# A long convolution by FFT ahead of a token-mixing layer: one weight load for all frequencies of the first transform, with x loads, spectrum loads, evictions and stores moved

## The chip, the cores and the metric

The kernel runs on one core of a Trainium2 chip. The metric is the device time of a whole run in microseconds (us). The five engines of the core work side by side: PE (TensorE, matmuls; PEld is its weight load), DVE (VectorE), ACT (ScalarE), POOL (GpSimd) and SP (SyncE, which here only issues DMAs). An *eviction* is the copy of a matmul's result out of PSUM, where PE writes it, into SBUF, the on-chip memory that the engines work from. A DMA *lands* when its data has arrived. The kernel before took 2326.43 us (median of 2 runs, 2326.23 to 2326.64).

## The reference

Two layers in a row. The first is a causal long convolution along the sequence; the second mixes tokens with two 5696 x 5696 matrices.

```python
batch, seq, d_model = 8, 5696, 128
# layer 1
L = 2 * S
y = irfft(rfft(x, n=L, axis=1) * rfft(h, n=L, axis=0)[None], n=L, axis=1)[:, :S, :]
# layer 2, with x = y
theta = x @ w_theta
zr, zi = x * cos(theta), x * sin(theta)
u = x + einsum('ts,bsd->btd', w_tok_r, zr) + einsum('ts,bsd->btd', w_tok_i, zi)
out = u + maximum(u @ w_ch, 0)
```

## The kernel before

The convolution is done by matmuls with Fourier tables, in eight *groups* (batch pair `bp`, channel half `dh`). For each group:

- **first transform** (`stage_a`): weights are the 128 sequence columns of one channel of x, the moving operand is the table `f1_t`; one half of the frequencies at a time;
- **second transform and product** (`f2`, `stage_b`): 12 chunks of frequencies, evicted by ACT, multiplied on DVE with the spectrum of h, which is loaded from HBM chunk by chunk (`hs`, four buffers);
- **inverse stage** (`stage_c`): 256 matmuls with a dense weight load each, evicted by DVE with a sign;
- **last stage** (`stage_d`): 128 matmuls, seven evictions on ACT, then the result goes to HBM.

`woven` interleaves lists of steps in program order. The first transform of group g+1 is woven into the inverse stage of group g; the product of group g+1 into the last stage of group g. Then 44 *phase steps* make zr and zi for layer 2, and a long matmul part mixes tokens.

```python
HALF = ((0, K1 // 2 + 1), (K1 // 2 + 1, K1 // 2 - 1))      # K1 = 90: 46 and 44 frequencies
fa = pool("fft_a", 2, ...);  fh = pool("fft_h", 4, ...)

def stage_a(lhs, kh, dst):                                  # for each half kh
    k0, kn = HALF[kh]
    def chunk(q):
        ...
        for i in range(8):
            nc.tensor.matmul(ps[:, i // 4, (i % 4) * 2 * kn:(i % 4 + 1) * 2 * kn],
                             lhs(q + i), f1_t[:NB, 2 * k0:2 * k0 + 2 * kn], start=True, stop=True)
        nc.scalar.activation(...)                           # eviction on ACT
    return [lambda q=q: chunk(q) for q in range(0, HD, 8)]

def lhs(q):                                                 # weights: every 128th element of a row of x16
    return x16.rearrange("p b n d -> p (b n) d")[:NB, :, dh * HD + q]

def stage_b(a_of, dh):
    def chunk(c):
        hs = fh.tile([P, 2, HD * CK], F16, tag="hs", name="hs")
        for e in range(2):
            nc.sync.dma_start(hs[64 * e:64 * e + 64], hf_hbm[dh, c])
        ps = f2(a_of, c)
        nc.scalar.activation(xs[:, :, :, :ck], ps, AF.Copy)
        for r in range(2):
            nc.vector.tensor_tensor(uv[r][:, :, :, k0:k0 + ck], xs[...], hv[:, r:r + 1, ...], op=mult)

for g, (bp, dh) in enumerate(groups):
    ...
    woven(stage_c(st), nxt, now)                            # nxt: first transform of g + 1
    if dh == 0 and bp + 1 < B // 2:
        x16s[bp + 1] = load_x(bp + 1)                       # Pool queue, one x buffer
    ...
    woven(stage_b(a_of, ...) if nxt else [], stage_d(st, bp, dh), now)

# phase step (phases_b): buffers red and mag, two of each
nc.scalar.activation(mag, r, AF.Abs)
nc.scalar.activation(red, r, AF.Sin, ...)
nc.scalar.activation(mag, mag, AF.Sin, ...)
zi_eng.tensor_mul(zi, red, yflat);  nc.vector.tensor_mul(zr, mag, yflat)
nc.sync.dma_start(...)                                      # two stores of zr, two of zi, one of y
```

Of the kernel before, what the change touches and what calls it, by code (L numbers as in the profile page):

```python
# [12 lines left out]
F16 = mybir.dt.float16  # L13
add = mybir.AluOpType.add
mult = mybir.AluOpType.mult
AF = mybir.ActivationFunctionType
# [6 lines left out]
def kernel(  # L23
# [68 lines left out]
    assert N1 * N2 == NF and NB * N2 == S and NB % 2 == 1 and K1 <= P  # L92
    HALF = ((0, K1 // 2 + 1), (K1 // 2 + 1, K1 // 2 - 1))
    CHK = [(kh, c0, min(CK, HALF[kh][1] - c0)) for kh in range(2) for c0 in range(0, HALF[kh][1], CK)]
    NCK = len(CHK) // 2
    CN = 10
    CHN = [(c0, min(CN, N2 - c0)) for c0 in range(0, N2, CN)]
    UVW = 2 * HD * K1
    hf_hbm = nc.dram_tensor("hf_hbm", (2, 2 * NCK, N2, 2, HD * CK), F16, kind="Internal").ap()
    yt_hbm = nc.dram_tensor("yt_hbm", (D, B, S), BF16, kind="Internal").ap()  # L100
# [13 lines left out]
    fc = pool("fft_c", 1, conv, side="right")  # L114
    fa = pool("fft_a", 2, conv, side="right")
    fs = pool("fft_s", 2, conv, side="right")
# [58 lines left out]
    t, k = turns_of([[1, K1]], 0, lane[:NB, 1:2], NB, N1)  # L175
    for k0, kn in HALF:
        sine(f1_t[:NB, 2 * k0 + kn:2 * k0 + 2 * kn], t[:, k0:k0 + kn], -1)
    for k0, kn in HALF:
        cosine(f1_t[:NB, 2 * k0:2 * k0 + kn], t[:, k0:k0 + kn], k[:, k0:k0 + kn])

# [9 lines left out]

    def stage_a(lhs, kh, dst):

        k0, kn = HALF[kh]
        st = {}

        def chunk(q):
            if q == 0:
                st["a"] = dst[kh] = fa.tile([P, 2 * HALF[0][1], HD], F16, tag="a", name="a_")
            ps = psum()
            for i in range(8):  # L200
                nc.tensor.matmul(ps[:, i // 4, (i % 4) * 2 * kn:(i % 4 + 1) * 2 * kn],  # L201
                                 lhs(q + i), f1_t[:NB, 2 * k0:2 * k0 + 2 * kn], start=True, stop=True)
            nc.scalar.activation(
                st["a"][:, :2 * kn, q:q + 8].rearrange("p k (a q) -> p k a q", a=2),
                ps[:, :, :8 * kn].rearrange("p a (q k) -> p k a q", q=4), AF.Copy)
        return [lambda q=q: chunk(q) for q in range(0, HD, 8)]

    def f2(a_of, c):

        kh, c0, ck = CHK[c]  # L210
        a_, (k0, kn) = a_of[kh], HALF[kh]
        ps = psum()
        for j in range(ck):
            for ri in range(2):
                for e in range(2):
                    rows = slice(64 * e, 64 * e + 64)
                    nc.tensor.matmul(ps[:, e, j * HD:(j + 1) * HD],  # L217
                                     w_t2[rows, k0 + c0 + j, N2 * (1 - ri):N2 * (3 - ri)],
                                     a_[rows, ri * kn + c0 + j, :],
                                     start=(ri == 0), stop=(ri == 1))  # L220
        return ps[:, :, :ck * HD].rearrange("p e (k d) -> p e d k", k=ck)

    def woven(*lists):

        steps = [((i + 0.5) / len(l), n, f) for n, l in enumerate(lists) for i, f in enumerate(l)]
        for _, _, f in sorted(steps, key=lambda s: s[:2]):
            f()
# [3 lines left out]
    x16s = {0: load_x(0)}  # L231
    a_h = {}
    woven([s for kh in range(2) for s in stage_a(
        lambda q: h16[:NB].rearrange("p h n d -> p (h n) d")[:, :, q], kh, a_h)],
        [lambda k0=k0: w_table(k0) for k0 in range(15, K1, 15)])

    hst = [t[:, :NCK * D * CK].rearrange("p (c h d k) -> p c h d k", c=NCK, h=2, k=CK) for t in (u_t, v_t)]
    for kh in range(2):
        nc.gpsimd.memset(hst[kh][:, NCK - 1], 0.0)

    def h_chunk(c):
        kh, c0, ck = CHK[c]
        ps = f2(a_h, c)
        dst = hst[kh][:, c % NCK, :, :, :ck]
        if c % 2:
            nc.vector.tensor_scalar(dst, ps, 16.0 / NF, None, op0=mult)  # L246
        else:
            nc.scalar.activation(dst, ps, AF.Copy, scale=16.0 / NF)
        for cc, j in ((0, 0), (2 * NCK - 1, CHK[-1][2] - 1)):
            if c == cc:  # L250
                nc.vector.tensor_scalar(dst[:, :, :, j], dst[:, :, :, j], 0.5, None, op0=mult)
        for ri in range(2):
            nc.sync.dma_start(
                hf_hbm[:, c, :, ri, :].rearrange("h p n -> p h n"),
                hst[kh][64 * ri:64 * ri + 64, c % NCK].rearrange("p h d k -> p h (d k)"))

    for c in range(2 * NCK):
        h_chunk(c)
# [32 lines left out]

    def stage_b(a_of, dh):

        def chunk(c):
            kh, c0, ck = CHK[c]
            hs = fh.tile([P, 2, HD * CK], F16, tag="hs", name="hs")
            hv = hs.rearrange("p r (d k) -> p r d k", k=CK)
            for e in range(2):
                nc.sync.dma_start(hs[64 * e:64 * e + 64], hf_hbm[dh, c])
            ps = f2(a_of, c)  # L300
            xs = fs.tile([P, 2, HD, CK], F16, tag="xs", name="xs")
            nc.scalar.activation(xs[:, :, :, :ck], ps, AF.Copy)  # L302
            k0 = HALF[kh][0] + c0
            for r in range(2):
                nc.vector.tensor_tensor(  # L305
                    uv[r][:, :, :, k0:k0 + ck], xs[:, :, :, :ck],
                    hv[:, r:r + 1, :, :ck].to_broadcast([P, 2, HD, ck]), op=mult)
        return [lambda c=c: chunk(c) for c in range(2 * NCK)]

# [16 lines left out]
    def stage_d(st, bp, dh):  # L326
        def chunk(n0, cn):
            if n0 == 0:
                st["yt"] = fg.tile([P, NB, N2], BF16, tag="yt", name="yt")
            g_, yt = st["g"], st["yt"]  # L330
            ps = psum()
            nq = 5 if cn == CN else cn
            for j in range(cn):
                n = n0 + j
                o = ps[:, j // nq, (j % nq) * NB:(j % nq + 1) * NB]
                for ri in range(2):
                    e_ = e_t[:K1, n, ri, :] if n < EN else e_t[:K1, N2 - n, ri, ::-1]
                    nc.tensor.matmul(o, g_[:K1, ri * N2 + n, :], e_, start=(ri == 0), stop=(ri == 1))
            nc.scalar.activation(  # L339
                yt[:, :, n0:n0 + cn].rearrange("p m (a q) -> p m a q", q=nq),  # L340
                ps[:, :cn // nq, :nq * NB].rearrange("p a (q m) -> p m a q", q=nq), AF.Copy)
            if n0 + cn == N2:
                for e in range(2):
                    nc.sync.dma_start(yt_hbm[dh * HD:(dh + 1) * HD, 2 * bp + e, :],
                                      yt[64 * e:64 * e + 64].rearrange("p m n -> p (m n)"))
        return [lambda n0=n0, cn=cn: chunk(n0, cn) for n0, cn in CHN]

    groups = [(bp, dh) for bp in range(B // 2) for dh in range(2)]

    def front(g):  # L350
        bp, dh = groups[g]
        a_of, x16 = {}, x16s[bp]

        def lhs(q):
            return x16.rearrange("p b n d -> p (b n) d")[:NB, :, dh * HD + q]
        return [s for kh in range(2) for s in stage_a(lhs, kh, a_of)], a_of

    a0, a_of = front(0)
    woven(a0, [lambda: r_table(0, r_u), lambda: r_table(1, r_v), s_table])
    woven(stage_b(a_of, 0), [lambda n0=n0: e_table(n0) for n0 in range(0, EN, 11)])  # L360
    setup.close()
    fg = pool("fft_g", 1, conv, side="right")

    def phases_b(ti, y_ap, b0, nb, yT, sb, th_pool, th_tag, zi_eng, turns=None, tags=("red", "mag"), m=P,
                 theta_ps=None):
        n = nb * D
# [36 lines left out]
        for r, (z, dst) in enumerate(((zr, zr_hbm), (zi, zi_hbm))):  # L403
            for e in range(2):
                t0 = ti * P + e * 64
                if t0 >= 2 * H:
                    if e == 0:
# [3 lines left out]
                i, t0 = divmod(t0, QR)  # L411
                nc.sync.dma_start(dst[p_, t0 // 64, i, :, b0 * D:b0 * D + n],
                                  z[e * 64:e * 64 + 64])
# [27 lines left out]
    def phase_step(ti, hh):  # L441
# [5 lines left out]
        for b in range(4):  # L447
# [4 lines left out]
                          y_ap.rearrange("p b d -> p (b d)"))  # L452
        phases_b(ti, y_ap, 4 * hh, 4, yT, st["sb1"], None, None, nc.vector, st["turns"], theta_ps=ps[:, 0, :])

# [5 lines left out]
    for g, (bp, dh) in enumerate(groups):  # L460
        st = {}
        last = g + 1 == len(groups)
        nxt, a_of = front(g + 1) if not last else ([], None)
        now = [steps0.pop(0) for _ in range(10)] if last else []
        woven(stage_c(st), nxt, now)
        if dh == 0 and bp + 1 < B // 2:
            x16s[bp + 1] = load_x(bp + 1)
        if g + 2 == len(groups):
# [3 lines left out]
        now = [steps0.pop(0) for _ in range(6)] if last else []  # L472
        woven(stage_b(a_of, groups[g + 1][1]) if nxt else [], stage_d(st, bp, dh), now)
    conv.close()
# [398 lines left out]
```

## Time and profile before

I cut the span into parts by the timeline (start of the first inverse matmul, its last, and so on). "Rest" is from the last inverse matmul of a group to the first one of the next: the last stage of one group with the product of the next.

| part, us | before |
|---|---|
| tables, spectrum of h, first product | 100.7 |
| inverse stages of groups 0 to 6 | 214.0 (30.5 each) |
| rests of groups 0, 2, 4 (x is loaded there) | 92.5 (30.8 each) |
| rests of groups 1, 3, 5, 6 | 84.9 |
| group 7 with 16 phase steps | 55.6 |
| last inverse-transform matmul to last of the 44 phase steps | 116.5 |
| last phase step to first sum of the mixing part | 57.5 |
| mixing part | 1605.4 |

From the page of the kernel before, the span and the chain of work that ended last (followed back from the last instruction, as shares of the span by engine and then by line):

```profile
span 2327.1 us, 42585 instructions
...
PE 62%; DMA 5%; DVE 4%; POOL 1%; issue 1%; ACT 1%; SPq 0%; DVEq 0%; ACTq 0%
PE m L812 56%; DMA wb<-in_moe_w_tok_r_dram 2%; POOL wb L534 1%; DVE c L819 1%; DMA wb<-in_moe_w_tok_i_dram 1%; DMA zr_hbm<-mag 1%; PE utp L624 1%; PE v L631 1%; PE m L773 1%; PE m L775 1%; PE m L816 1%; DVE wt L543 1%; DMA y_hbm<-yb 1%; DMA
```

The chain says that the mixing matmuls, L812, hold 56% of the span. The change leaves them alone, so the whole gain must come from the first 671 us.

Groups of instructions of the kernel before in its first 560 us (line, engine, operation, tiles, shape, count | busy us, mean ns | idle time before them and who ended it). L201 is the first transform, L320 half of the inverse stage, L305 the product:

```profile
L201 PE MATMUL ps<-f_t,x 89*128 89x88 f16 (+1 forms) x1024 | 144.7, 302 | 1.1 <-DVE v_t L246 1.0
L320 PE MATMUL ps<-r_u,u_t 128*128 128x128 f16 x1024 | 140.5, 229 | 33.6 <-DVE u_t L305 32.7 <-ACT red L396 0.3
...
L201 PEld LDWEIGHTS <-x 89*128 89x128 f16 x1024 | 136.7, 269 | 1.3 <-issue 1.1
...
L305 DVE TENSOR_TENSOR u_t<-xs,hs 128x1024 f16<-128x1024 f16 x96 | 63.9, 666 | 67.2 <-DMA hs<-hf_hbm 46.1 <-ACT xs L302 18.9 <-ACT yt L339 1.2
```

1024 loads of x keep the weight path busy for 136.7 us, 133 ns each. (The means, 269 and 302 ns, are of single overlapping instructions; busy time over count tells the pace.)

The timeline around one forward step of the kernel before (start us, duration us, instruction, count):

```profile
167.99 1.08 PEld L201 LDWEIGHTS <-x 89*128 89x128 f16 x8
168.04 1.15 PE L201 MATMUL ps<-f_t,x 89*128 89x92 f16 x8
168.24 1.35 DVE L322 TENSOR_TENSOR g__2515<-ps,sgn 90x1024 f16<-90x1024 f32 x1 [0.23 <-PE ps L321]
...
169.87 0.36 PEld L201 LDWEIGHTS <-x 89*128 89x128 f16 x2
```

Eight loads take 1.08 us without a gap. The next forward step begins 1.88 us after this one: 16 inverse matmuls, 55 ns apart, fill the rest.

Windows of the kernel before (stretch, its length, busy us and instructions of each engine, PE clock that was granted as a share of full speed, DMA share, GB/s): the inverse stage of group 2, its rest, and the phase steps alone:

```profile
core 0: us, PE busy (x) PEld busy (x) DVE busy (x) ACT busy (x) POOL busy (x), PEclk, DMA share, GB/s
213.30:243.70 30.40, 30.40 (x377) 30.25 (x378) 21.84 (x16) 11.57 (x15) 0.00 (x0) 0.94 0.28 75
243.70:274.40 30.70, 17.02 (x499) 15.45 (x497) 15.54 (x25) 16.68 (x20) 2.10 (x4) 0.67 0.82 175
583.00:660.00 77.00, 47.44 (x311) 31.78 (x310) 42.72 (x76) 40.16 (x67) 0.00 (x0) 0.63 0.58 151
```

In the inverse stage PE is busy for all of 30.4 us. In the rest no engine is: DVE works 15.5 of 30.7 us. Who made DVE wait in that rest (engine, line, releaser: us, times, longest):

```profile
DVE u_t L305 <- DMA hs<-hf_hbm: 12.3, 2, 10.6
```

DVE stood still for 10.6 us at once for a spectrum chunk, while the x load (20 us to land, issued just as the stage began) was in the DMA engines.

Timeline of SP and ACT in the kernel before, in two phase steps:

```profile
597.62 1.18 SPq L412 DMA_DIRECT2D zr_hbm<-mag  x2
...
598.46 0.60 ACT L395 ACTIVATE mag<-ps 128x512 f32<-128x512 f32 x1 [2.30 <-DMA zr_hbm<-mag]
...
598.86 0.59 SPq L412 DMA_DIRECT2D zi_hbm<-red  x1
...
599.49 1.09 SPq L451 DMA_DIRECT2D y_hbm<-y_ap  x2
...
600.37 0.60 ACT L395 ACTIVATE mag<-ps 128x512 f32<-128x512 f32 x1
600.62 0.44 SPq L652 DMA_DIRECT2D yy<-y_hbm  x1
...
601.16 1.09 SPq L412 DMA_DIRECT2D zi_hbm<-red  x2
```

SP issues without a pause, about 0.6 us for each DMA. At 598.46 ACT has waited 2.30 us for a store of zr to land and give back its buffer.

### The profile page before, as it was taken

To read this page: it belongs to the slowest core of one execution; us is meant where nothing else is said; L and a number is where in the kernel's file an instruction comes from. 1 tells how busy PE (TensorE), PEld (TensorE's weight loads), DVE (VectorE), ACT (ScalarE), POOL (GpSimd) and SP (SyncE) were. 2 spreads that over 40 slices of the span, in tenths; PEclk is the share of its full clock that TensorE was granted. 3 is DMA by queue.
4 is the path that set the end of the run, shared out by engine and by line. 5 is a ranking of instruction groups with operands and counts; after the bars stand their busy time and mean duration, and the time that the engine had idled before them with its cause. 6 is when DMAs were issued, how large, how long until landed. Compare 5 with 4: busy or idle time off the path is not lost.

```text
span 2327.1 us, 42585 instructions
## 1 busy us (share of the span) xinstructions
PE 2080.3 (89%) x16255; PEld 1187.5 (51%) x16255; DVE 1693.7 (73%) x3004; ACT 633.8 (27%) x931; POOL 842.6 (36%) x1521
## 2 busy tenths in 40 slices
PE   3778787875558999999999999799999999999997
PEld 3778787863333444444444444244444444444443
DVE  5757675774579888886888767787767777777674
ACT  5645454554532233322331000011111111111111
POOL 3300000002014445445455664345454454444540
PEclk9889798997679999999999999899999999999998
DMA  5252525358588999988999987968797787877972
GB/s 126 81 131 82 131 82 131 82 158 203 145 259 145 175 179 176 169 169 145 173 171 172 162 130 163 262 103 143 132 157 130 138 153 132 151 139 133 156 128 57
DMA packets 408989, 340.47 MB, mean 146 GB/s; under 512 B 83759, under 2 KB 366255, under 8 KB 406959
## 3 DMA queue, kind: packets, MB, share of 16 engines
q0 software_dynamic: 218240, 143.00, 45.6%
q1 hardware_dynamic: 183440, 179.41, 26.9%
q10 hardware_dynamic: 7104, 15.34, 1.9%
q8 instruction: 127, 2.08, 0.4%
q14 instruction: 78, 0.64, 0.1%
HBM read 382.55 MB, written 97.93 MB: 206 GB/s over the span
## 4 chain that ended last, share of the span: by engine, by line
PE 62%; DMA 5%; DVE 4%; POOL 1%; issue 1%; ACT 1%; SPq 0%; DVEq 0%; ACTq 0%
PE m L812 56%; DMA wb<-in_moe_w_tok_r_dram 2%; POOL wb L534 1%; DVE c L819 1%; DMA wb<-in_moe_w_tok_i_dram 1%; DMA zr_hbm<-mag 1%; PE utp L624 1%; PE v L631 1%; PE m L773 1%; PE m L775 1%; PE m L816 1%; DVE wt L543 1%; DMA y_hbm<-yb 1%; DMA b<-zr_hbm 0%; PE theta_ps L375 0%
## 5 line engine op out<-in xcount | busy, mean ns | idle before, releaser
L534 POOL DMA_DIRECT2D wb<-in_moe_w_tok_i_dram x720 | 389.9, 553 | 816.1 <-DVE wt L543 734.1
L534 POOL DMA_DIRECT2D wb<-in_moe_w_tok_r_dram x720 | 389.0, 556 | 305.3 <-ACT yt L339 188.6
L812 PE MATMUL m<-b,wt 128*128 128x512 bf16 x1936 | 454.4, 381 | 19.6 <-DVE wt L543 15.6
L543 DVE STREAM_TRANSPOSE wt<-wb 128x384 f32<-128x384 f32 (+2 forms) x720 | 359.4, 522 | 129.2 <-PE m L812 68.0
L812 PEld LDWEIGHTS <-wt 128*128 128x128 bf16 x1936 | 189.3, 98 | 254.5 <-DVE wt L543 18.6
L819 DVE TENSOR_TENSOR c<-c,m 128x512 f32<-128x512 f32 x440 | 283.2, 668 | 0.0
L626 ACT ACTIVATE uts<-utp 128x512 bf16<-128x512 bf16 (+1 forms) x90 | 53.3, 592 | 616.2 <-PE utp L624 616.2
L320 PE MATMUL ps<-r_u,u_t 128*128 128x128 f16 x1024 | 140.5, 229 | 33.6 <-DVE u_t L305 32.7
L201 PE MATMUL ps<-f_t,x 89*128 89x88 f16 (+1 forms) x1024 | 144.7, 302 | 1.1 <-DVE v_t L246 1.0
L321 PE MATMUL ps<-r_v,v_t 128*128 128x128 f16 x1024 | 137.9, 228 | 0.3
L201 PEld LDWEIGHTS <-x 89*128 89x128 f16 x1024 | 136.7, 269 | 1.3 <-issue 1.1
L320 PEld LDWEIGHTS <-u_t 128*128 128x128 f16 x1024 | 110.5, 108 | 33.8 <-DVE u_t L305 33.8
L621 ACT ACTIVATE ub<-c 128x512 bf16<-128x512 f32 (+1 forms) x90 | 56.5, 628 | 226.7 <-DMA wb<-in_moe_w_tok_i_dram 163.4
L305 DVE TENSOR_TENSOR u_t<-xs,hs 128x1024 f16<-128x1024 f16 x96 | 63.9, 666 | 67.2 <-DMA hs<-hf_hbm 46.1
L321 PEld LDWEIGHTS <-v_t 128*128 128x128 f16 x1024 | 106.5, 104 | 3.2 <-issue 1.9
L135 POOL DMA_DIRECT2D x<-in_x_dram x16 | 8.6, 542 | 266.5 <-PE ps L201 266.2
L302 ACT ACTIVATE xs<-ps 128x1024 f16<-128x1024 f32 x96 | 91.5, 986 | 48.7 <-DVE v_t L305 43.6
L217 PEld LDWEIGHTS <-w_t 64*128 64x128 f16 x3240 | 65.2, 105 | 45.8 <-issue 22.8
L575 ACT ACTIVATE yb<-tpz 128x512 bf16<-128x512 bf16 (+1 forms) x46 | 27.5, 597 | 166.2 <-PE tpz L573 133.1
L633 DVE SCALAR_TENSOR_TENSOR c<-v,c 128x512 f32<-128x512 f32 (+1 forms) x90 | 61.4, 682 | 11.1 <-PE v L631 8.6
L377 ACT ACTIVATE red<-theta_ps,magic 128x512 f32<-128x512 f32 (+1 forms) x46 | 31.6, 687 | 135.3 <-PE theta_ps L375 115.7
L305 DVE TENSOR_TENSOR v_t<-xs,hs 128x1024 f16<-128x1024 f16 x96 | 64.9, 676 | 0.0
(2848 smaller groups left out, 3840.6 us busy)
## 6 DMA issues: line engine op xcount, KB each, us to landing
wb<-in_moe_w_tok_r_dram POOLq DMA_DIRECT2D x352, 96.0 KB, 4.5
wb<-in_moe_w_tok_i_dram POOLq DMA_DIRECT2D x352, 96.0 KB, 4.8
wb<-in_moe_w_tok_r_dram POOLq DMA_DIRECT2D x352, 80.0 KB, 4.4
wb<-in_moe_w_tok_i_dram POOLq DMA_DIRECT2D x352, 80.0 KB, 3.8
hs<-hf_hbm SPq DMA_DIRECT2D x192, 128.0 KB, 3.2
cp_hbm<-c SPq DMA_DIRECT2D x88, 256.0 KB, 2.3
c<-cp_hbm SPq DMA_DIRECT2D x88, 256.0 KB, 4.4
out_dram<-c SPq DMA_DIRECT2D x88, 256.0 KB, 4.3
```

The costliest lines, as they stand in the source:

```text
L201: nc.tensor.matmul(ps[:, i // 4, (i % 4) * 2 * kn:(i % 4 + 1) * 2 * kn], lhs(q + i), f1_t[:NB, 2 * k0:2 * k0 + 2 * kn], start=True, stop=True)
L217: nc.tensor.matmul(ps[:, e, j * HD:(j + 1) * HD], w_t2[rows, k0 + c0 + j, N2 * (1 - ri):N2 * (3 - ri)], a_[rows, ri * kn + c0 + j, :], sta ...
L302: nc.scalar.activation(xs[:, :, :, :ck], ps, AF.Copy)
L305: nc.vector.tensor_tensor(uv[r][:, :, :, k0:k0 + ck], xs[:, :, :, :ck], hv[:, r:r + 1, :, :ck].to_broadcast([P, 2, HD, ck]), op=mult)
L320: nc.tensor.matmul(o, u_t[:, at:at + P], r_u, start=True, stop=False)
L321: nc.tensor.matmul(o, v_t[:, at:at + P], r_v, start=False, stop=True)
L534: nc.gpsimd.dma_start(wb[32 * i:32 * i + 32, :ng, :nj * 64], bass.AP(tensor=a.tensor, offset=a.offset + row0 * S + p * H + i * QR + j0 * 6 ...
L543: nc.vector.transpose(wt.rearrange("p j t r -> p (j t r)").bitcast(F32).rearrange("p (j g t) -> p g j t", j=TJ, g=4)[:, :ng, :nj], wb[:, : ...
L621: nc.scalar.activation(ub[:m].rearrange("p b d -> p (b d)"), c[:m], AF.Copy)
L633: nc.vector.scalar_tensor_tensor(c[:m], v[:m], 0.0, c[:m], op0=ALU.max, op1=ALU.add)
L812: nc.tensor.matmul(ms[q], a[q][:, j, :, r], bts[jj][q][:, r, :], start=(jj == 0 and r == 0), stop=(jj == NJ - 1 and r == 1 and q not in left))
L819: nc.vector.tensor_tensor(c, z, ms[q], op=op)
```

## The change

The intent: halve the weight loads of the first transform by streaming all 180 columns (real and imaginary, 90 frequencies) through each; load x earlier, by squeezing the forward steps into the first 70% of the inverse stage; issue spectrum loads four chunks ahead; move two of seven evictions of the last stage to DVE; and take the stores of zr in phase steps off the SP queue.

```diff
-    HALF = ((0, K1 // 2 + 1), (K1 // 2 + 1, K1 // 2 - 1))
-    CHK = [(kh, c0, min(CK, HALF[kh][1] - c0)) for kh in range(2) for c0 in range(0, HALF[kh][1], CK)]
+    CHK = [(c0, min(CK, K1 - c0)) for c0 in range(0, K1, CK)]
...
-    fa = pool("fft_a", 2, conv, side="right")
+    fa = pool("fft_a", 1, conv, side="right")
...
-            for i in range(8):
-                nc.tensor.matmul(ps[:, i // 4, (i % 4) * 2 * kn:(i % 4 + 1) * 2 * kn],
-                                 lhs(q + i), f1_t[:NB, 2 * k0:2 * k0 + 2 * kn], start=True, stop=True)
+            for i in range(4):
+                nc.tensor.matmul(ps[:, i // 2, (i % 2) * 2 * K1:(i % 2 + 1) * 2 * K1], lhs(q + i), f1_t[:NB],
+                                 start=True, stop=True)
+            if both and q % 8:                    # for h: every other eviction on DVE
+                nc.vector.tensor_copy(a_out, a_in)
+            else:
+                nc.scalar.activation(a_out, a_in, AF.Copy)
...                                               # stage_b: LEAD = 4
+        def load(c):
+            hs = hs_of[c] = fh.tile([P, 2, HD * CK], F16, tag="hs", name="hs")
+            for e in range(2):
+                nc.sync.dma_start(hs[64 * e:64 * e + 64], hf_hbm[dh, c])
         def chunk(c):
...
+            load(c + LEAD)
...                                               # stage_d
-            nc.scalar.activation(yt[...], ps[...], AF.Copy)
+            if n0 in (CHN[2][0], CHN[5][0]):
+                nc.vector.tensor_copy(y_out, y_in)
+            else:
+                nc.scalar.activation(y_out, y_in, AF.Copy)
...                                               # phases_b
-                nc.sync.dma_start(dst[p_, t0 // 64, i, :, b0 * D:b0 * D + n],
+                (z_eng if r == 0 else nc.sync).dma_start(dst[p_, t0 // 64, i, :, b0 * D:b0 * D + n],
                                   z[e * 64:e * 64 + 64])          # z_eng=nc.gpsimd in phase_step
...                                               # loop over groups
-        woven(stage_c(st), nxt, now)
         if dh == 0 and bp + 1 < B // 2:
-            x16s[bp + 1] = load_x(bp + 1)
+            def next_x(bp=bp):
+                x16s[bp + 1] = load_x(bp + 1)
+            woven(c_, (a_ + [next_x], 0.7), now, load_)
+        else:
+            woven(c_, a_, now, load_)
```

## The prediction

> **What bounds the kernel now.** The timeline splits the span (2327.1 us) in three: table setup and spectrum of h (to about 64 us), eight transform groups with the first phase steps (64 to 548, then phase steps alone to 671), and the token-mixing matmuls (first at 671, last at 2289 us). The change doesn't touch the last 1656 us, which are matmul-bound (chain of waits: PE 62%, its main matmul line 56%). All gain must come from the first 671 us.
>
> *Inverse stage.* By the timeline each of groups 0 to 6 spends 30.5 us from its first to its last inverse matmul. It is PE-bound: windows of it show PE 99% busy, DVE 70%, ACT 38%. One of its 16 steps lasts 1.88 us: 16 inverse matmuls at 55 ns (0.88) plus 8 forward ones at 134 ns. The 134 ns is the weight load of strided x (eight loads fill 1.07 us without a gap), not the 92-column matmul. The change streams all 180 columns per load: half as many loads; the longer matmul should stay hidden under the load. (The Trainium skill, "TensorE: Matmul & The Clock Gate", part 2, says that the PE pulls weight loads ahead of running matmuls; the trace agrees: loads are back to back, 134 ns apart.) PE falls to about 0.88 + 4 x 0.134 = 1.42 us a step. The DVE eviction (mean 1.36 to 1.51 us a group) becomes the co-limiter, so I expect 1.5 us a step, 24 us a stage; 25 where the forward steps are squeezed to 70%. Seven stages: **-42 us**.
>
> *Product/last stage.* It takes 20.6 us where no x load runs, 30.9 in groups 0, 2 and 4: there the x load (issued as the stage starts, 20 us to land) holds up the spectrum loads (DVE idle 11.7 us at once, released by the spectrum DMA). The change issues x at about 68% of the inverse stage, some 7 us earlier, and four spectrum chunks are resident (they mostly were before). x then still lands about 14 us into the stage, so I expect 26 us, not 20: **-15 us** in three groups. Two evictions of seven move from ACT (17.2 us) to DVE (15.5 to 17.4): balance only, with the spectrum prefetch **-4 us** over the rest.
>
> *h and first x transform.* Half of h's evictions go to DVE, and loads halve: **-6 us**.
>
> *Phase steps.* From 583 to 660 us the SP queue issues stores back to back, 0.6 us each, 3.1 us a step, and ACT (2.0 us a step) waits for the zr stores to land. Moving two of five stores to Pool leaves SP 1.9 us, but two buffers and the landing keep a step near 2.7: -9 us over 22 steps. Against it: instruction order puts the 24 early weight loads of the last stage among the zr stores on the in-order Pool queue, so some stores wait behind weights around 548 to 575, much as DMA contention delays them now. (The Trainium skill, "DMA: Bandwidth & Descriptors", "Issuing engines are not separate DMA queues": another issuer saves sequencer time only. Here that is the limit.) With the last group: **-12 us**.
>
> Sum -79: **2248 us, range 2220 to 2276**. Faster by over 2%: 0.93; within 2%: 0.06; slower: 0.01.
>
> **Right if:** inverse stage 24 us with DVE over 90% busy and the wide matmul still 134 ns per load; stages with x about 26, with the DVE still waiting on spectrum loads; phase step below 3 us; last stage unchanged.
>
> **Wrong if:** the 180-column matmul doesn't hide under the load; DVE evictions slow down; x now delays the next forward transform; Pool stores queue behind weight loads (phase stage longer); or the first mixing matmuls wait for late weights.

## The result, and the profile after

The changed kernel took 2256.66 us (median of 2 runs, 2253.44 to 2259.89), against 2326.43 before. The ratio is 0.97, with a 95% interval from 0.964 to 0.976. (Ratios are the mean time of one kernel's fast runs over that of the other's of the same rounds, so not quite the ratio of the medians.) All runs quoted in this document were fast, that is, within 1.5% of the fastest of the same kernel.

| part, us | before | after | difference | predicted |
|---|---|---|---|---|
| tables, spectrum of h, first product | 100.7 | 95.6 | -5.1 | -6 |
| inverse stages 0 to 6 | 214.0 | 170.4 | -43.6 | -42 |
| rests 0, 2, 4 | 92.5 | 81.5 | -11.0 | -15 |
| rests 1, 3, 5, 6 | 84.9 | 86.1 | +1.2 | -4 |
| group 7 | 55.6 | 50.5 | -5.1 | } |
| to the last phase step | 116.5 | 117.4 | +0.9 | } -12 |
| to the first mixing sum | 57.5 | 50.4 | -7.1 | } |
| mixing part | 1605.4 | 1605.9 | +0.5 | 0 |

The same groups in the kernel after (L197 is the first transform, L309 the product):

```profile
L325 PE MATMUL ps<-r_u,u_t 128*128 128x128 f16 x1024 | 141.8, 232 | 30.6 <-DVE u_t L309 28.8 <-ACT red L404 0.9 <-DVE g__8273 L327 0.5
...
L197 PE MATMUL ps<-f_t,x 89*128 89x180 f16 x512 | 87.4, 308 | 1.7 <-ACT xs L307 0.9 <-DVE turn L160 0.4 <-DVE v_t L243 0.4
L197 PEld LDWEIGHTS <-x 89*128 89x128 f16 x512 | 74.4, 239 | 2.5 <-issue 1.9
...
L309 DVE TENSOR_TENSOR u_t<-xs,hs 128x1024 f16<-128x1024 f16 x96 | 65.0, 677 | 35.7 <-ACT xs L307 17.5 <-DMA hs<-hf_hbm 17.3 <-ACT yt L349 0.5
```

512 loads now take 74.4 us, 145 ns each, so a load with a 180-column matmul behind it costs hardly more than one with 92 columns (133 ns).

The timeline around a forward step of the kernel after:

```profile
199.87 0.58 PEld L197 LDWEIGHTS <-x 89*128 89x128 f16 x4
199.93 0.69 PE L197 MATMUL ps<-f_t,x 89*128 89x180 f16 x4
200.13 1.22 DVE L327 TENSOR_TENSOR g__3310<-ps,sgn 90x1024 f16<-90x1024 f32 x1 [0.72 <-PE ps L326]
```

Four loads take 0.58 us. Before, eight took 1.08.

Windows of the kernel after, again the inverse stage of group 2, its rest, and the phase steps alone:

```profile
193.80:217.80 24.00, 24.00 (x318) 23.72 (x318) 17.48 (x15) 11.01 (x15) 2.10 (x4) 0.89 0.53 122
217.80:244.20 26.40, 15.71 (x491) 14.23 (x489) 18.64 (x29) 14.82 (x17) 0.00 (x0) 0.85 0.83 178
539.40:598.00 58.60, 36.50 (x235) 24.90 (x240) 42.23 (x75) 31.52 (x54) 19.43 (x38) 0.59 0.69 199
```

The inverse stage shrank from 30.4 to 24.0 us, and PE is still busy for all of it. DVE is busy for 17.5 of 24.0 us, 73%; its evictions also got shorter (mean 1.21 to 1.32 us a group, before 1.21 to 1.51). This is a stage with squeezed forward steps, though. The steady part of one without (group 1; columns as above) looks like this:

```profile
156.00:172.00 16.00, 16.00 (x228) 16.00 (x226) 14.90 (x13) 8.69 (x12) 0.00 (x0) 1.00 0.10 30
```

DVE is busy there for 93% of the time, close to its limit but not at it: an eviction takes 1.32 us, and by the starts of the inverse matmuls a step lasts 1.42 us, which is just the prediction's sum for PE (0.88 + 4 x 0.134). The stage is longer than 16 such steps (22.7 us) because of its start. From 148.4 to 153.2 us the granted clock was 0.50, the inverse matmuls followed each other every 107 ns instead of every 55, and the first three steps took 2.5, 2.3 and 2.0 us. Each inverse stage of groups 0 to 6, in both kernels, has 3 to 6 us at half the clock.

DMA traffic has moved into the inverse stage of group 2 (share 0.53 after, 0.28 before): that is the x load. The waits of DVE in the rest of group 2:

```profile
DVE u_t L309 <- DMA hs<-hf_hbm: 5.7, 1, 5.7
```

From 12.3 to 5.7 us: the x load still lands inside this stage, but earlier in it.

Timeline of SP, POOL and ACT in two phase steps of the kernel after:

```profile
549.13 0.60 ACT L403 ACTIVATE mag<-ps 128x512 f32<-128x512 f32 x1 [2.44 <-DMA zr_hbm<-mag]
...
551.00 0.60 ACT L403 ACTIVATE mag<-ps 128x512 f32<-128x512 f32 x1
551.06 1.09 SPq L420 DMA_DIRECT2D zi_hbm<-red  x2
...
551.93 1.04 POOL L420 DMA_DIRECT2D zr_hbm<-mag  x2 [3.15 <-DVE mag L410]
...
552.25 0.53 SPq L459 DMA_DIRECT2D y_hbm<-y_ap  x1
...
554.90 0.60 ACT L403 ACTIVATE mag<-ps 128x512 f32<-128x512 f32 x1 [2.12 <-DMA zr_hbm<-mag]
```

SP has pauses now. But ACT still waits for the landing of zr, 2.44 us, then 2.12. From one such wait to the next is 5.77 us for two steps. On average the phase steps alone did not get shorter: over the last 23 steps one took 3.34 us (start to start on ACT), before 3.37.

### The profile page after: what moved, and what is told of

Same layout as the page of the kernel before. It is cut to its first block, busy times and chain, and to the rows that moved or that the text cites. A ratio compares the mean times of both kernels' runs of the same rounds, so it can differ in the third digit from the quotient of the medians.

```text
span 2257.7 us, 41296 instructions
## 1 busy us (share of the span) xinstructions
PE 2017.7 (89%) x15504; PEld 1136.4 (50%) x15679; DVE 1691.5 (75%) x3027; ACT 612.9 (27%) x905; POOL 880.7 (39%) x1608
## 4 chain that ended last, share of the span: by engine, by line
PE 62%; DVE 4%; DMA 4%; issue 2%; POOL 1%; ACT 0%; SPq 0%; DVEq 0%; ACTq 0%; POOLq 0%
PE m L825 57%; DMA wb<-in_moe_w_tok_i_dram 2%; DVE c L832 2%; POOL wb L547 1%; DMA wb<-in_moe_w_tok_r_dram 1%; PE utp L637 1%; PE v L644 1%; PE m L786 1%; PE m L788 1%; DVE wt L556 1%; PE m L829 1%; PE theta_ps L383 0%; PE tpz L586 0%; DMA b<-zr_hbm 0%; DMA zr_hbm<-mag 0%
## 5 line engine op out<-in xcount | busy, mean ns | idle before, releaser
L325 PE MATMUL ps<-r_u,u_t 128*128 128x128 f16 x1024 | 141.8, 232 | 30.6 <-DVE u_t L309 28.8
L420 POOL DMA_DIRECT2D zr_hbm<-mag x88 | 46.2, 529 | 226.5 <-DVE mag L410 214.6
L307 ACT ACTIVATE xs<-ps 128x1024 f16<-128x1024 f32 x96 | 92.1, 977 | 58.4 <-DVE v_t L309 21.3
L215 PEld LDWEIGHTS <-w_t 64*128 64x128 f16 x3240 | 66.2, 106 | 55.6 <-issue 30.3
L309 DVE TENSOR_TENSOR u_t<-xs,hs 128x1024 f16<-128x1024 f16 x96 | 65.0, 677 | 35.7 <-ACT xs L307 17.5
L197 PE MATMUL ps<-f_t,x 89*128 89x180 f16 x512 | 87.4, 308 | 1.7 <-ACT xs L307 0.9
L197 PEld LDWEIGHTS <-x 89*128 89x128 f16 x512 | 74.4, 239 | 2.5 <-issue 1.9
```

The source lines that it names most:

```text
L197: nc.tensor.matmul(ps[:, i // 2, (i % 2) * 2 * K1:(i % 2 + 1) * 2 * K1], lhs(q + i), f1_t[:NB], start=True, stop=True)
L215: nc.tensor.matmul(ps[:, e, j * HD:(j + 1) * HD], w_t2[rows, c0 + j, N2 * (1 - ri):N2 * (3 - ri)], a_st["a"][rows, ri * K1 + c0 + j, :], s ...
L309: nc.vector.tensor_tensor(uv[r][:, :, :, c0:c0 + ck], xs[:, :, :, :ck], hv[:, r:r + 1, :, :ck].to_broadcast([P, 2, HD, ck]), op=mult)
L325: nc.tensor.matmul(o, u_t[:, at:at + P], r_u, start=True, stop=False)
```

## The experiments

The theories, in short. A: the first transform ran at the pace of its weight loads, which are slow because the columns are strided, and halving their number is nearly all of the gain; the rival is a cost of switching between the kinds of step. B: the phase steps are held by the landing of zr and two buffers, so that the moved stores gave nothing by themselves; the rival is that the full SP queue held them. C: the product starves for spectrum while x lands, so that the place of the x load counts; the rival is that the earlier issue of the spectrum loads does it. D: the evictions moved to DVE cost a little; the rival is that they balance the two engines.

"The base" is the changed kernel timed again, in the first run below. Differences are of medians. The kernel before was run beside each call; its medians over four calls were 2326.31 to 2327.97 us, so a difference between calls is uncertain by about 2 us from the chip, and the base itself spreads over 6 us.

### The base again

> The changed kernel again, for its spread and as the base of the other runs: 2253 to 2260 us as in its first two runs. Differences of other runs under about 4 us should not be read from single times.

Measured: 2255.67 us (5 runs, 2251.45 to 2257.60); ratio to the kernel before 0.9691 [0.9674, 0.9707].

### Each load streams half of the columns again

```diff
-                nc.tensor.matmul(ps[:, i // 2, (i % 2) * 2 * K1:(i % 2 + 1) * 2 * K1], lhs(q + i), f1_t[:NB], ...)
+                for r in range(2):
+                    o = (i % 2) * 2 * K1 + r * K1
+                    nc.tensor.matmul(ps[:, i // 2, o:o + K1], lhs(q + i), f1_t[:NB, r * K1:r * K1 + K1], ...)
```

> The changed kernel with the wide matmul cut in two again: each strided column of x is loaded as weights twice, and each load streams 90 columns. All else stays. Theory A (the inverse stage gained because half of the strided weight loads went): inverse stages of groups 0 to 6 go back from 24.4 to about 30.5 us, PE over 97% busy, total about 2300 us (+43). Rival (it gained from the new order of steps, the single buffer of the first transform or the eviction shape): inverse stages stay under 27 us, total under 2275 us.

Measured: 2316.74 us, +61.1. The weight loads of x in this run:

```profile
L199 PEld LDWEIGHTS <-x 89*128 89x128 f16 x1024 | 135.7, 270 | 3.4 <-issue 2.9
```

The pace is that of the kernel before (135.7 us for 1024). The inverse stages took 218.8 us in all, in the base 168.0: +50.8, or 7.3 us each. The first part took 105.0 instead of 95.3 us. Theory A holds; the expectation of +43 left out most of what h and the first group pay (+9.7), and each stage came back a little longer than it had been before (31.3 instead of 30.6 us). The other parts of the change together, without this one, are worth only 10 us (2316.74 against 2326.75).

### Dense weights in the kernel before (wrong on purpose)

```diff
-            return x16.rearrange("p b n d -> p (b n) d")[:NB, :, dh * HD + q]
+            return x16.rearrange("p b n d -> p (b n d)")[:NB, (dh * HD + q) * P:(dh * HD + q + 1) * P]
```

> The kernel before, wrong on purpose: the forward weights are 128 adjacent elements of x instead of every 128th one; as many loads, of the same size, with the same 92- and 88-column matmuls. Theory A2 (the 134 ns of a forward step is the stride of its weight load): loads fall to 55 to 65 ns, the inverse stage to 22 to 25 us and the total by 40 us or more. Rival (a load of 128 columns into 89 rows, or a switch between the two kinds of step, costs 134 ns however the weights lie): inverse stage stays at 30 us.

Measured: 2245.60 us, -80.7 against the kernel before (2326.31). The results are wrong, as meant, and only the time is used. The group of its loads of x:

```profile
L201 PEld LDWEIGHTS <-x 89*128 89x128 f16 x1024 | 57.8, 107 | 0.9 <-issue 0.4
```

The window of its inverse stage of group 2 (columns as above):

```profile
184.60:205.80 21.20, 21.20 (x379) 21.20 (x380) 18.38 (x16) 11.57 (x15) 0.00 (x0) 0.90 0.41 103
```

The same number of loads, of the same shape, under the same matmuls, now takes 57.8 us: 56 ns each instead of 133. (From start to start inside a run of loads the median is 40 ns, before 120; 40 is also the pace of the matmuls behind them, so the dense load itself may be faster still.) The inverse stages fall to 149.6 us, 21.4 each. Their limit is now DVE. Its evictions in the same stage, ten without a gap:

```profile
188.82 12.25 DVE L322 TENSOR_TENSOR g__3567<-ps,sgn 90x1024 f16<-90x1024 f32 x10 [0.64 <-PE ps L321]
```

A step lasts 1.21 to 1.23 us there, as long as an eviction (1.22 us), with PE's own sum (0.88 + 8 x 0.040 = 1.20) barely below. PE counts as busy all the time, which alone does not show that PE is the limit. The eviction itself depends on the loads: the same instruction took 1.21 to 1.22 us in stages with dense or no loads of x, 1.22 to 1.33 with 64 strided ones, and 1.32 to 1.62 with 128 (means of a group, this run, the changed kernel and the run above among them). Why is not shown.

So the load was slow because its 128 columns lie 256 bytes apart. The Trainium skill, "SBUF — State Buffer", section "Door 1: The DMA port swizzle", says that SBUF has 16-byte lines, and that each access which crosses to a new line pays a penalty; a step of 256 bytes crosses at every element. The measured factor of 2.4 agrees with the direction. No run here varied the stride in steps, so the rule itself is not shown here. The rival, that every switch between kinds of step costs this, falls: the weave was the same.

### x loaded after the inverse stage again

```diff
-            def next_x(bp=bp):
-                x16s[bp + 1] = load_x(bp + 1)
-            woven(c_, (a_ + [next_x], 0.7), now, load_)
+            woven(c_, a_, now, load_)
+            x16s[bp + 1] = load_x(bp + 1)
```

> The changed kernel with the x load back behind the inverse stage and its forward steps spread over all of that stage; the spectrum loads stay issued ahead. Theory C (the gain of 11 us in the last stages of groups 0, 2 and 4 comes from x being issued about 7 us earlier): these stages go back from 26 to 30 us or more, the inverse stages stay at 24, total +9 to +14 us. Rival (the gain there comes from the spectrum loads issued ahead): within 3 us of the changed kernel.

Measured: 2264.64 us, +9.0. The rests of groups 0, 2 and 4 took 92.6 us, exactly as before the change (92.5), in the base 82.1; the inverse stages stayed (168.9, base 168.0). The waits of DVE in the rest of group 2:

```profile
DVE u_t L309 <- DMA hs<-hf_hbm: 11.5, 2, 11.2
```

With the spectrum loads still issued ahead, the wait is back at 11.5 us. Theory C holds: it is the place of the x load that counts. (The edit also spreads the forward steps over the whole stage again; the stages did not change their length by it.) What issuing the spectrum loads ahead by the same four buffers gave is not measured by a run of its own; this run leaves no room for it in these rests.

### Six spectrum buffers

```diff
-    fh = pool("fft_h", 4, conv, side="right")
+    fh = pool("fft_h", 6, conv, side="right")
-    LEAD = 4
+    LEAD = 6
```

> The changed kernel with six spectrum buffers instead of four, and six chunks loaded ahead. Theory C (in groups 0, 2 and 4 the product steps starve for spectrum while x lands, idle 5.75 us at once): two more resident chunks cover 2.8 us each time, 6 to 10 us in all. Rival (they would wait for something else right behind it): within 3 us.

Measured: 2249.64 us, -6.0. The rests of groups 0, 2 and 4 took 77.7 us (base 82.1). The wait for spectrum in group 2 fell to 2.5 us (5.7 in the first run of the changed kernel). That fits theory C. The total alone would not show it: -6.0 us is the spread of the base, and the intervals of the two ratios overlap (0.9658 to 0.9685, base 0.9674 to 0.9707). Eight buffers did not fit into SBUF; that kernel does not build.

### All phase stores on SP again

```diff
-        phases_b(..., theta_ps=ps[:, 0, :], z_eng=nc.gpsimd)
+        phases_b(..., theta_ps=ps[:, 0, :])
```

> The changed kernel with all phase stores back on the SP queue. Theory B (two buffers bound the step as tightly as the SP queue does, so the moved stores bought next to nothing by themselves): within 4 us of the changed kernel, about 2252 to 2260 us. Rival (the Pool stores are what shortened the stretch from the last inverse stage to the first mixing results, some 6 to 12 us): 2262 us or more.

Measured: 2264.54 us, +8.9, so theory B falls in this form: the moved stores are worth about 9 us. But not in the phase steps alone, which took 116.9 us here and 116.7 in the base. Group 7 got 3.1 us longer (53.8 against 50.7), and the stretch from the last phase step to the first mixing sum 6.1 (55.7 against 49.6). The instruction order shows what may lie behind the latter. In the order of the SP queue of the changed kernel, eight of the large loads for the mixing part (tile b, 512 KB each) stand before the zi stores of the 37th phase step; with all stores on SP, and in the kernel before, four do. By the times of landing, 9 such loads had landed by the last phase step in the kernel after, 6 in this run, 6 in the kernel before. Three loads more to wait for, at the 223 GB/s of the window after it, are 3 x 524,288 bytes / 223 GB/s = 7.1 us (an estimate from these numbers). That fits, but no run moved these loads alone: it is argued, not shown. The other traces agree only in part. All four runs with the stores on SP took 55.7 to 59.7 us for this stretch, and nine of the ten with them on Pool 48.7 to 51.1; but the tenth ("The two together" below) took 54.6 us with 8 loads landed, where two others with 8 took 48.7. So the number of landed loads is not the whole cause.

### A third buffer in the phase steps, after and before

```diff
-        mag = sb.tile([P, n], F32, tag=tags[1], name="mag")[:m]
+        mag = sb.tile([P, n], F32, tag=tags[1], name="mag", bufs=None if turns is None else 3)[:m]
```

> The changed kernel with a third buffer for the cosine product that the moved stores read. Theory B (with two buffers, the phase steps alone are bound by the recycling of that buffer: compute 2.8 us, then two stores issued 0.5 us apart, then 2.0 to 2.4 us to land, 5.9 us for two steps): step falls from about 3.0 to 2.3 us, total 12 to 18 us less than the changed kernel. Rival (DMA bandwidth or the SP queue bounds the phase steps): less than 4 us.

> The kernel before with the same third buffer. Theory B' (before, the SP queue with five stores a step at 0.6 us each bounds the phase steps as well, at 3.1 us, so a buffer alone buys nothing): total within 4 us of 2326. Rival (only the buffer bound it before, the queue was never a limit): 12 us or more faster.

Measured: the changed kernel with it 2240.82 us, -14.9. The kernel before with it 2329.84 us, against 2326.75 without: ratio 1.0018 [1.0004, 1.0032], if anything slower. The phase steps alone took 105.7 us after (base 116.7) and 121.8 before (116.5). Who made ACT wait in that part of the base (engine, tile, line, releaser: us, times, longest):

```profile
ACT mag L403 <- DMA zr_hbm<-mag: 40.8, 15, 9.1
```

The same view of the changed kernel with the third buffer:

```profile
ACT mag L403 <- PE ps L400: 21.0, 12, 3.1
...
ACT mag L403 <- DMA zr_hbm<-mag: 1.3, 1, 1.3
```

The wait for zr went from 40.8 to 1.3 us; a wait for PE took part of its place, so a step took 2.99 us (mean over the last 23 steps by the timeline; 3.30 in the base), not the 2.3 expected. The pair of runs shows that the buffer pays only in the changed kernel: there it was the limit, and in the kernel before it was not the only one. That the SP queue was the other is argued from the trace: in the phase steps of the kernel before with the third buffer, SP spent 69.8 of 86 us issuing (changed kernel with it: 41.7 of 78), and ACT waited 35.5 us for PE where it had waited for zr. The run that would show it, the changed kernel with all stores on SP and the third buffer, was not made.

### All last evictions on ACT

```diff
-            if n0 in (CHN[2][0], CHN[5][0]):
+            if False:
```

> The changed kernel with all seven evictions of the last inverse matmuls back on ACT. Theory D (two evictions at 1.08 us each on DVE, where ACT took 0.93, gained nothing, since DVE is the busier engine of that stage: 17.7 us of 21.1): last stages 0.3 to 1 us shorter or the same, total within 6 us, rather faster than the changed kernel. Rival (ACT was the limit there, as the change seems to have supposed): each last stage gets about 1 us longer, total +5 to +8 us.

Measured: 2249.94 us, -5.7. The rests of groups 1, 3, 5, 6 took 84.0 us (base 86.5, kernel before 84.9). This speaks for theory D, that this part of the change cost a little. Only half of the 5.7 us shows in these rests; the other half is no larger than the spread of the base (6 us), so the size of this cost is uncertain, and the intervals of the ratios overlap (0.9659 to 0.9693, base 0.9674 to 0.9707).

### Dense weights with right results

The Pool engine is idle in the groups. It copies four columns of x at a time into a dense tile (four buffers of 1 KB a partition), and the weights are loaded from there:

```diff
+            xt = fy.tile([P, 4, 2 * N2], F16, tag="xt", name="xt")
+            nc.gpsimd.tensor_copy(xt[:NB], lhs(slice(q, q + 4)).rearrange("p m q -> p q m"))
+            w = lambda i: xt[:NB, i - q]
...
-                nc.tensor.matmul(..., lhs(q + i), f1_t[:NB], start=True, stop=True)
+                nc.tensor.matmul(..., w(q + i), f1_t[:NB], start=True, stop=True)
```

> The changed kernel, with the idle Pool engine copying four columns of x at a time into a dense tile, from which the weights are loaded. Right results. Theory A2 (the stride is the cost of the weight load): a forward step falls from about 140 ns to 75 to 85 ns, now bound by its 180 columns, and the inverse stage from 24 to about 22 us, then bound by the DVE evictions (16 of 1.25 to 1.3 us); total -10 to -17 us against the changed kernel. Rival: Pool's copies [...]come too late or slow the DVE[...]: inverse stage 24 us or longer.

Measured: 2250.54 us, only -5.1, within the spread of the base. The inverse stages did fall as expected, from 168.0 to 149.2 us (21.3 each). But the first inverse stage started only at 110.9 us, instead of 95.3: in the first group nothing hides the copies, and Pool is busy with tables then. The gain of 18.8 us was mostly given back there. DVE's evictions took 1.22 us beside the copies, no longer than without them (1.22 in the run with wrong results), so the rival that Pool slows DVE falls; in the steady part of a stage without squeezed steps DVE was busy for all of 13 us, as expected.

### The two together

The edit is that of the dense weights, and three buffers for both `red` and `mag`:

```diff
-        sb1 = pool("s2", 2, pha, reuse_waits="tile")
+        sb1 = pool("s2", 3, pha, reuse_waits="tile")
```

> The dense weights and a third buffer for both products of the phase step, in one kernel. If both gains are real and apart: about 2255 - 15 - 13 = 2227 us, range 2218 to 2238; the phase steps, then bound by ACT at 2.0 us or by the SP queue at 1.9, near 2.3 us.

Measured: 2237.93 us, within the stated range, at its slow end. The dense weights had given only 5 us by themselves, not the 13 assumed, and a phase step took 3.05 us, not 2.3.

### The parts that paid, in one kernel

The dense copies for groups 1 to 7 only, the third buffer for `mag`, all last evictions on ACT:

```diff
-        steps, a_st = stage_a(lambda q: x16[:NB, :, dh * HD + q])
+        dense = g > 0
+        steps, a_st = stage_a(lambda q: x16[:NB, :, dh * HD + q.start:dh * HD + q.stop] if dense else
+                              x16[:NB, :, dh * HD + q], dense=dense)
```

> The changed kernel with the dense weight copies on Pool for groups 1 to 7 only (in the run that also made them for the first group, the first inverse stage started at 110.7 instead of 95.3 us), the third buffer for the cosine product and all last evictions on ACT. If the three parts are independent: the first inverse stage starts at 95 us again, inverse stages of 20.5 to 22 us, phase part as with the third buffer alone; about 2255.7 - 15 - 18 - 5 = 2218 us, range 2210 to 2228. If the Pool copies cost the other engines anything, 2228 or more.

Measured: 2219.98 us (5 runs, 2218.41 to 2222.50), results right; ratio to the kernel before 0.9540 [0.9527, 0.9553], where the changed kernel has 0.9691. It beats both kernels. Two groups of its instructions, the copies on Pool and the weight loads from the dense tile:

```profile
L199 POOL COPY xt<-x 89x512 f16<-89x512 f16 x112 | 125.2, 1138 | 179.3 <-PE ps L203 117.3 <-DMA x<-in_x_dram 37.3 <-PE ps L221 18.3
...
L203 PEld LDWEIGHTS <-xt 89*128 89x128 f16 x448 | 37.4, 102 | 2.2 <-issue 2.0
```

448 dense loads take 37.4 us, 83 ns each. With half as many columns behind each, the dense loads of the run with wrong results took 56 ns, so it is now the 180 columns that set this pace. The first inverse stage starts at 99.5 us, 4 us later than in the base; the copies for group 1 are likely the reason, but no run shows it.

## Why the prediction was right, point by point

The measured 2256.66 us lies in the range, 8.7 us above the stated 2248.

- **Inverse stage: right, the exact size in part by luck.** Predicted -42 us, measured -43.6. Halving the strided loads is the cause: undoing only that gave back 50.8 us in these stages. "24 us a stage" was measured at 23.8 to 24.8. But the prediction got from its own sum for PE, 1.42 us a step, to 1.5 by a limit on DVE. The steady step was 1.42; the rest of the 24 us is the start of the stage at half the clock, which the prediction did not have. The page that the prediction cites ("TensorE: Matmul & The Clock Gate", part 2) agrees with the trace in that loads run back to back while matmuls run.
- **"The DVE eviction becomes the co-limiter": close, but it did not limit.** Without squeezing, DVE was busy for 93% of the steady part, with it for 73% of the stage; the step stayed PE's. The evictions had become shorter than the means that the prediction read from the kernel before (1.32 us at most, not 1.36 to 1.51), because they, too, depend on the number of strided loads. With dense weights DVE did become the limit, at 1.22 us a step.
- **x load: right mechanism, gain too high.** Predicted -15, measured -11.0. Two of the three rests took 26.4 and 26.2 us, as said; the first took 28.9. The runs with x late and with six buffers fit that DVE starves for spectrum while x lands.
- **The other rests, -4: wrong, +1.2.** The step "balance only, with the spectrum prefetch" was mis-sized. The two evictions took 1.08 us each on DVE, which was the busier engine there, and the run with them back on ACT was 2.5 us shorter in these rests, 5.7 in all (uncertain by the base's spread). In that run the rests took 84.0 us, before 84.9, so the earlier spectrum loads gave at most about 1 us here. Why the move cost anything is open: with the evictions back, ACT was the busier engine (17.8 of 20.8 us, DVE 16.1), and the rest was still shorter.
- **Phase steps and last group: -12 predicted, -11.3 measured, but for another reason; the number is luck.** "A step near 2.7" did not come (3.34 us; "right if" said below 3): the steps alone took 117.4 us instead of 116.5. I had put the recycling of two buffers at 5.4 us for two steps; it is 5.8 to 5.9 (compute 2.8, then two stores half a microsecond apart, and up to 2.5 us to land), and beside it the mixing part's early loads now ran among the steps. The gain came in group 7 (-5.1) and behind the last step (-7.1). The run with the stores back on SP shows that 9 us of it belong to the moved stores. The cited sentence of "DMA: Bandwidth & Descriptors", that another issuer saves only sequencer time, is not contradicted: moving the stores took issue time off SP and saved nothing in the steps alone, and what it saved elsewhere is not traced to one cause.
- **h and first transform: right**, -5.1 against -6.

Part by part, by undoing each in the changed kernel: the wide matmul 61 us, the early x load 9, the Pool stores 9, the DVE evictions -6 (within the spread of the base). The sum is 73; the whole change was 71 (2326.75 to 2255.67).

## What to carry to other kernels

Where a small matmul runs at the pace of its weight load, look at the stride of the weights first; the profile shows this case as loads back to back. Here a dense copy by an idle engine, and more columns behind each load, both took cost away. Then look for the next limit by the length of one step, not by the busy share: with the dense weights PE still counted as busy for 100% of the stage, but it was DVE that had no gap left. When two limits lie close together, such as an issue queue and a pair of buffers, lifting one shows nothing; test each with the other lifted. A large transfer can starve a stage that lives on small loads once its prefetched pieces are used up (10.6 us at once here): move it earlier, or deepen the prefetch.

## What the Trainium skill lacked or had wrong

- "TensorE: Matmul & The Clock Gate", section "LDWEIGHTS": it gives about columns / 1.2 ns, which is 107 ns for 128 columns, and names no layout; the table of fast weight loads in the section after it gives the read pattern as "packed or strided", without a difference in cost. Here 128 f16 columns took 56 ns dense and 133 ns at a step of 256 bytes, at the same shape. The page lacks what the stride costs.
- "DMA: Bandwidth & Descriptors", section "Issuing engines are not separate DMA queues": it calls the sequencer's time "usually small relative to the DMA itself". That holds for one DMA here (about 0.6 us to issue, medians of 2.0 to 2.9 us to land in the kernel before). It lacks that issue times add up on one queue: five 64 to 128 KB stores a step kept SP for about 3.1 us, longer than the 2.0 us that ACT worked on it. Moving two of them was worth 8.9 us in all, though none of it in the steps alone.
- "GPSIMD Engine Reference", section "7. Performance pitfalls for Q7 kernels": about 2.9 cycles an element for reads with a step of more than 8 bytes. The copy of 512 f16 elements a partition at a step of 256 bytes took 1069 ns (median), 2.1 ns an element with its fixed cost. That is about 2.5 cycles, an estimate with the 1.2 GHz which the skill's "Trainium Kernel Development and Optimization", "NeuronCore Architecture", gives for that engine. The page's figure stands among costs of kernels written for that engine's cores, and this was its ordinary copy, so the two need not be the same.
